# Range checks moved to GpSimd bytes, a searched instruction order, and fewer halved output tiles in a fused attention and mixture kernel

## The chip, the core and the metric

The kernel runs on one core of a Trainium2 chip. The core has TensorE (PE; its weight loads are listed as PEld), VectorE (DVE), ScalarE (ACT), GpSimd (POOL), and SyncE (SP), on whose queue nearly all transfers are issued. The metric is device time of one execution in microseconds (us), lower is better. All arithmetic that matters here is float32, or fp32r on TensorE.

## What is computed

Three layers run one after the other: attention with two kinds of mask, a soft mixture of eight experts, and a layer `g = h - tanh(h)` between two weight matrices.

```python
# attention: 4 batches, 8 heads, 576 tokens, head size 64; x becomes [2304, 512]
scores = where(mask[h], q @ k.T / 8, -1e9);  x = softmax(scores) @ v
# soft mixture: 8 experts, 4 slots each
logits = x @ phi                              # [2304, 32]
slot_input = softmax(logits, axis=0).T @ x    # [32, 512]
slot_out[e] = relu(slot_input[e] @ w1[e]) @ w2[e]
x = softmax(logits, axis=1) @ slot_out        # [2304, 512]
# last layer
h = x @ w_in                                  # 2304 x 2048
out = (h - tanh(h)) @ w_out                   # 2304 x 512
```

All inputs are stored as 64-bit floats, so a piece of 128 by 512 weights is a load of 512 KB and has to be narrowed on the chip.

## The kernel before

The work lies in three stretches. **Attention** runs first (up to about 121 us). While it runs, half of the last layer's weights (eight pieces of `w_in`, called i0 to i7, and eight of `w_out`, o0 to o7) are loaded and narrowed. **Dispatch, experts and combine** follow (to about 181 us); they stream the expert weights through recycled buffers. `dispatch` ends with two PSUM copies into `ct` (L745, L746) on DVE, and behind them on DVE stand the two copies of the slot inputs (L1295) for which the first expert matmul waits.

The **second stage** (`second`, L876) is the last layer. The output of the mixture is a product of a 2304 by 32 matrix `cT` and `soT`, so for each of 16 blocks `f` of the hidden layer it makes a small factor `Gs` (L974 to L992), then `h = Gs * cT` for a group of up to four 128-token tiles (L1106), then on ACT a square `u` (L1110), then the polynomial `r = (h + b) * u`. That is one DVE instruction (L1117), or, for a third of the blocks (`POOLR`), an ACT copy `d` (L1121) and a GpSimd product (L1125). Each tile then adds `r * wh[f]` to its PSUM accumulator (L1079). A further matmul of `cT` with the matrix `Ms` is added once per tile (`affine`). `Ms` needs every piece of `w_out`.

Tiles 0 to 17 are grouped as A (0 to 3), BG (4 to 7), C (8 to 11), DG (12 to 15), EG (16, 17). The list `phases` (L879) says in which order groups are worked, over which blocks, and where their sums go. `"part"` copies the accumulator of the first eight blocks to SBUF (`store`, L1156). `"add"` adds it to the second half on DVE (L1174). `"out"` is a plain copy by ACT or DVE (L1168). Before the change A, BG and EG are worked in halves, which is ten tiles.

The remaining 16 pieces (`loads`) arrive during the second stage. Each is narrowed by `low` (ACT L269 or GpSimd L271), `top` (GpSimd L274) and `merge` (DVE L279). Once the last one is merged, all 32 pieces are loaded **again** (L1259), only to find out whether any exponent was outside the range for which the fast path is right: `check` (L896) is one DVE instruction for each piece, on the top 16 bits of 512 elements, and a last `sift`, a matmul `marks` and some tiny DVE instructions (`judge_*`) make a flag. If the flag is set, a slow general path runs behind the end; with these inputs it doesn't. The buffers of raw pieces are 12 (`RAW`).

The order of instructions on every engine in the second stage is not written by hand. `Plan.run` (L91) is a list scheduler: each task has an engine and an estimated duration, the scheduler takes among the tasks that could start first the one with the longest chain behind it, and the emitted order is the order of estimated start times. Transfers of pieces are a task of an engine "DMA", output writes one of an engine "OUT"; the queue of SP on which both are issued is not a resource of its own. There are 3 PSUM buffers for `h`, 4 accumulators, 3 `u`, 2 `d`, and 5 `r`.

Of the kernel before, what the change touches and what calls it, by code (L numbers as in the profile page):

```python
# [13 lines left out]
I16 = mybir.dt.int16  # L14
BF16 = mybir.dt.bfloat16
# [26 lines left out]
WROUND = 2.0 ** -15 - 0.5  # L42
WHUGE = float(np.uint32(1151 << 20).view(np.float32))
# [33 lines left out]

class Plan:
# [12 lines left out]
    def run(self, free_at):  # L91
        tasks, free_at = self.tasks, dict(free_at)
        users, users_left, left, order, released = [[] for _ in tasks], [0] * len(tasks), {}, {}, {}
# [6 lines left out]
        for tag, keys in self.ordered.items():  # L100
            for k in range(self.bufs[tag], len(keys)):
                t = takes[tag, keys[k]]
                t["deps"] = t["deps"] + [g for g in gives[tag, keys[k - self.bufs[tag]]] if g not in t["deps"]]
        for t in tasks:
            t["dur"] = min(sum(p[1] for p in a) for a in t["alts"])
            for d in t["deps"]:
                users[d["id"]].append(t)
            users_left[t["id"]] = len(t["deps"])
            for x in t["free"]:
                left[x] = left.get(x, 0) + 1  # L110
        sorted_, wait = [t for t in tasks if not t["deps"]], list(users_left)
        for t in sorted_:
            for u in users[t["id"]]:
                wait[u["id"]] -= 1
                if not wait[u["id"]]:
                    sorted_.append(u)
        assert len(sorted_) == len(tasks)
        for t in reversed(sorted_):
            t["rank"] = t["dur"] + max((u["rank"] + 0.2 for u in users[t["id"]]), default=0.0)
        open_, emits, taken = [t for t in tasks if not t["deps"]], [], {}  # L120

        def after(d, t):
            if d["eng"] == t["alts"][0][0][0]:
                return 0.0 if d["eng"] == "PE" else 0.05
            return 0.35 if d["eng"] == "PE" else 0.15

        def earliest(t):
            s = t["ready"]
            for d in t["deps"]:
                s = max(s, d["end"] + after(d, t))  # L130
            for tag, key in t["take"]:
                k = order.get(tag, [])
                if tag in self.ordered and self.ordered[tag][len(k)] != key:
                    return None
                s = max(s, taken.get(tag, -99.0))
                if len(k) >= self.bufs[tag]:
                    old = (tag, k[len(k) - self.bufs[tag]])
                    if old not in released:
                        return None
                    s = max(s, released[old] + 0.2)  # L140
            return s

        while open_:
            found = []
            for t in open_:
                s = earliest(t)
                if s is None:
                    continue
                best = None
                for a in t["alts"]:  # L150
                    x, at = s, []
                    for eng, dur, _ in a:
                        x = max(x, free_at[eng])
                        at.append(x)
                        x += dur + 0.15
                    if best is None or x < best[0]:
                        best = (x, a, at)
                found.append((best[2][0], t, best))
            assert found, "no task can start"
            first = min(f[0] for f in found)  # L160
            s, t, (x, a, at) = max((f for f in found if f[0] <= first + 0.06), key=lambda f: f[1]["rank"] + f[1]["boost"])
            for (eng, dur, emit), b in zip(a, at):
                free_at[eng] = b + dur
                emits.append((b, len(emits), emit))
            t["end"], t["eng"] = at[-1] + a[-1][1], a[-1][0]
            for tag, key in t["take"]:
                order.setdefault(tag, []).append(key)
                taken[tag] = at[0]
            for x in t["free"]:
                left[x] -= 1  # L170
                t.setdefault("frees", []).append(x)
                self.ends = getattr(self, "ends", {})
                self.ends[x] = max(self.ends.get(x, 0.0), t["end"])
                if not left[x]:
                    released[x] = self.ends[x]
            open_.remove(t)
            for u in users[t["id"]]:
                users_left[u["id"]] -= 1
                if not users_left[u["id"]]:
                    open_.append(u)  # L180
        assert all("end" in t for t in tasks)
# [13 lines left out]
def attention_moe_moe(ctx: ExitStack, tc: tile.TileContext, q, k, v, phi, w1, w2, w_in, w_out, cst, out, dbg=None):  # L195
# [489 lines left out]
    def dispatch(pa, ps, ct):  # L685
# [59 lines left out]
        nc.vector.tensor_copy(ct[:, 0:4].rearrange("p c b s -> p c (b s)"), tps[:, 0:4])  # L745
        nc.vector.tensor_copy(ct[0:64, 4].rearrange("p b s -> p (b s)"), tps[0:64, 4])  # L746
# [129 lines left out]
    def second(raw, chk, cT, store, more, wh0):  # L876
# [9 lines left out]
        seen = chk.tile([128, 512], U16, name="seen")  # L886
        counted = []
# [4 lines left out]
        def check(piece):  # L892
            if not counted:
                nc.vector.tensor_scalar(out=seen, in0=quarter(piece, 3, U16), scalar1=0x7800, scalar2=0x3800, op0=ALU.bitwise_and, op1=ALU.bitwise_xor)
            else:
                nc.vector.scalar_tensor_tensor(out=seen, in0=quarter(piece, 3, U16), scalar=0x3800, in1=seen, op0=ALU.bitwise_xor, op1=ALU.bitwise_or)  # L896
            counted.append(piece)
# [23 lines left out]
        plan = Plan(dict(raw=RAW, h=3, p=1, acc=4, u=3, r=5, d=2, g1=2, o=8))  # L921
# [6 lines left out]
        DMA = 1.36  # L928
        for x in PRE:
            P["ld", x] = P["mg", x] = add(one("DMA0", 0.0, lambda: None), ready=-99.0)  # L930
        for k, piece in enumerate(PRE + loads):
# [7 lines left out]
            else:  # L939
                ld = add(one("DMA", DMA, lambda piece=piece: load(piece)), take=[("raw", piece)], ready=at - 1)  # L940
                ld = add(one("DMA0", 0.0, lambda: None), deps=[ld], ready=0)
# [3 lines left out]
            if k >= 0:  # L945
                lo = add(one("ACT", 0.88, lambda piece=piece: low(piece, True)), one("POOL", 1.1, lambda piece=piece: low(piece, False)), deps=[ld] + busy)
            if k >= 0:
                tp = add(one("POOL", 0.87, lambda piece=piece: top(piece)), deps=[ld] + busy)
            if k < 0:
                mg = P["ld", piece]  # L950
            else:
                mg = add(one("DVE", 0.85, lambda piece=piece: merge(piece)), deps=[ld, lo, tp], free=[("raw", piece)])
            P["mg", piece] = mg
            if kind == "o":
# [3 lines left out]
                P["wh", f] = add(one("POOL", 1.1, lambda f=f: nc.gpsimd.tensor_scalar(out=whi(f), in0=place(("o", f)), scalar1=8.0, scalar2=0.0, op0=ALU.mult, op1=ALU.add)),  # L958
# [493 lines left out]
```

## Time and profile before

| | us |
|---|---|
| median of the runs (3 runs) | 306.13 (305.60 to 306.23) |
| the profiled execution, device time | 307.51 |
| its span, first to last instruction | 305.7 |
| around the span | 1.8 |

| engine | busy us | share of the span |
|---|---|---|
| PE | 280.3 | 92% |
| DVE | 223.8 | 73% |
| ACT | 153.3 | 50% |
| POOL | 150.3 | 49% |

Shares are of the whole span, over three stretches with different limits, so they don't say which engine holds a stretch. A matmul's recorded duration is longer than the distance between the starts of two in a row, so PE's busy time overstates its work and hides some of its idle time. In a timeline row, the number in brackets is the idle time of the engine before the row, and behind the arrow is what ended it. A row with a count and one duration is a run of like instructions, first start to last end.

### The profile page before, as it was taken

The numbers are of one execution on the slowest core, as the hardware profiler recorded it, in microseconds if no ns is written. First come the engines' busy times: TensorE is split into PE (matmuls) and PEld (weight loads), VectorE is DVE, ScalarE is ACT, GpSimd is POOL, SyncE is SP. The second block draws the span as 40 slices with busy tenths as digits, with TensorE's granted clock in tenths as the row PEclk, the third lists the DMA queues.
The fourth block names the chain that finished last, engine by engine and source line by source line (L and its number), as shares of the span: only waits on it lengthen the run. The fifth ranks groups of instructions, "written<-read, shape, count | busy, mean of one in ns | idle before, by whom it ended". The sixth has DMA issues, their size and how long they took to land.

```text
span 305.7 us, 7472 instructions
## 1 busy us (share of the span) xinstructions
PE 280.3 (92%) x2684; PEld 193.4 (63%) x2684; DVE 223.8 (73%) x720; ACT 153.3 (50%) x289; POOL 150.3 (49%) x215
## 2 busy tenths in 40 slices
PE   5999999999899999989999876999999999998980
PEld 2688877878578877643333223677746787776750
DVE  5567988775979886526513109999999989999990
ACT  3356646546264455402212038797767348767530
POOL 8627957856789570010634028899370323323310
PEclk9999999999999999999999999999999999999997
DMA  7979899979897989999999999986471399984004
GB/s 206 249 200 347 236 341 307 346 219 300 261 352 207 346 289 399 411 407 373 385 408 409 407 393 397 409 280 207 144 209 61 90 390 396 383 324 139 0 0 147
DMA packets 62698, 86.94 MB, mean 284 GB/s; under 512 B 19008, under 2 KB 48064, under 8 KB 62656
## 3 DMA queue, kind: packets, MB, share of 16 engines
q1 hardware_dynamic: 61568, 86.15, 81.1%
q8 instruction: 23, 0.38, 0.5%
q10 hardware_dynamic: 1088, 0.26, 0.4%
q14 instruction: 19, 0.16, 0.2%
HBM read 81.67 MB, written 4.72 MB: 283 GB/s over the span
## 4 chain that ended last, share of the span: by engine, by line
PE 53%; DVE 15%; DMA 15%; POOL 5%; issue 5%; ACT 4%; SPq 1%; ACTq 0%; POOLq 0%; DVEq 0%
PE acc L1079 17%; PE sc L465 6%; PE pv L495 4%; PE h L1106 4%; PE pp L484 4%; DMA X<-in_moe_w 3%; DMA w<-in_moe_w 3%; DMA raw_o<-in_moe_w_out 3%; DVE seen L896 3%; DVE r L1117 3%; DMA raw_i<-in_moe_w_in 3%; PE xt L410 2%; PE hp L821 2%; PE tr_q L393 2%; PE tr_k L393 2%
## 5 line engine op out<-in xcount | busy, mean ns | idle before, releaser
L1079 PE MATMUL acc<-wh,r 128*128 128x512 f32 x288 | 79.6, 397 | 2.6 <-DVE r L1117 2.1
L1110 ACT ACTIVATE u<-h,co 128x512 f32<-128x512 f32 (+1 forms) x80 | 50.3, 648 | 26.9 <-PE h L1106 23.1
L1079 PEld LDWEIGHTS acc<-wh,r 128*128 128x128 f32 x288 | 52.7, 188 | 15.6 <-POOL X L274 1.9
L1125 POOL TENSOR_TENSOR r<-d,u 128x512 fp32r<-128x512 f32 (+1 forms) x22 | 27.6, 1255 | 49.6 <-PE acc L1079 25.5
L1117 DVE SCALAR_TENSOR_TENSOR r<-h,co,u 128x512 fp32r<-128x512 f32 (+1 forms) x58 | 38.6, 691 | 0.3
L465 PE MATMUL sc<-kT,qT 64*64 64x96 f32 (+1 forms) x608 | 34.2, 252 | 0.7 <-DVE kT L402 0.4
L469 DVE CUSTOM_DVE_ANT_0 sm<-sc,m_sb 128x96 f32<-128x96 f32 x144 | 29.2, 257 | 6.3 <-PE sc L465 6.2
L485 ACT ACTIVATE pT<-pp 96x512 f32<-96x512 f32 x38 | 23.1, 607 | 19.3 <-PE pp L484 19.3
L1106 PE MATMUL h<-cT,Gs 128*128 128x512 f32 (+1 forms) x80 | 29.6, 392 | 3.3 <-DVE r L1117 1.8
L465 PEld LDWEIGHTS sc<-kT,qT 64*64 64x64 f32 x608 | 26.9, 133 | 5.1 <-issue 1.8
L360 POOL TENSOR_SCALAR vw<-vw 32x256 f32<-32x256 f32 (+1 forms) x40 | 27.1, 678 | 4.6 <-DMA vw<-in_v 1.9
L495 PE MATMUL pv<-vw,pT 97*64 97x65 f32 x608 | 26.1, 227 | 0.1
L495 PEld LDWEIGHTS pv<-vw,pT 97*64 97x64 f32 x608 | 20.8, 137 | 7.7 <-issue 6.3
L403 ACT COPY qT<-tr_q 128x512 f32<-128x512 f32 x16 | 13.6, 851 | 23.6 <-PE tr_q L393 23.6
L484 PE MATMUL pp<-c_sb,sm 128*96 128x128 f32 x152 | 23.7, 278 | 1.5 <-DVE sm L473 0.9
L473 DVE TENSOR_TENSOR sm<-sm,mx 128x384 f32<-128x384 f32 (+1 forms) x38 | 22.5, 591 | 1.2
L1106 PEld LDWEIGHTS h<-cT,Gs 128*128 128x128 f32 x80 | 14.8, 188 | 13.5 <-DVE r L1117 6.7
L419 ACT COPY xT<-xt 128x512 f32<-128x512 f32 (+1 forms) x19 | 14.0, 758 | 11.5 <-PE xt L410 10.9
L484 PEld LDWEIGHTS pp<-c_sb,sm 128*96 128x96 f32 x152 | 15.8, 126 | 5.9 <-DVE sm L473 2.1
L274 POOL TENSOR_SCALAR pre<-raw_o 128x512 bf16<-128x512 int16 x16 | 13.7, 859 | 10.2 <-DMA raw_o<-in_moe_w_out 9.9
L279 DVE SCALAR_TENSOR_TENSOR pre<-raw_o,pre 128x512 int32<-128x512 int32 x16 | 13.8, 869 | 5.2 <-POOL pre L271 5.2
L896 DVE SCALAR_TENSOR_TENSOR seen<-raw_o,seen 128x512 uint16<-128x512 uint16 x16 | 17.3, 1080 | 0.3
(214 smaller groups left out, 484.5 us busy)
## 6 DMA issues: line engine op xcount, KB each, us to landing
w<-in_moe_w SPq DMA_DIRECT2D x54, 512.0 KB, 9.6
raw_i<-in_moe_w_in SPq DMA_DIRECT2D x32, 512.0 KB, 7.2
raw_o<-in_moe_w_out SPq DMA_DIRECT2D x32, 512.0 KB, 6.4
q<-in_q SPq DMA_DIRECT2D x16, 256.0 KB, 5.0
k<-in_k SPq DMA_DIRECT2D x16, 256.0 KB, 5.2
X<-in_moe_w SPq DMA_DIRECT2D x8, 512.0 KB, 9.4
out<-X SPq DMA_DIRECT2D x14, 256.0 KB, 4.2
vw<-in_v SPq DMA_DIRECT2D x16, 144.0 KB, 4.9
```

The source lines that it names most:

```text
L360: copy = lambda dst, src: nc.gpsimd.tensor_scalar(out=dst, in0=src, scalar1=1.0, scalar2=0.0, op0=ALU.mult, op1=ALU.add)
L465: nc.tensor.matmul(dst[half, lo:hi], lhsT=qT[u % NQ][half, i:i + QB], rhs=keys[half], start=True, stop=True)
L469: nc.vector.tensor_tensor_reduce(out=sm[:, o:o + n, :].rearrange("p g k -> p (g k)"), in0=sc[:, o:o + n, :].rearrange("p g k -> p (g k)"), ...
L484: nc.tensor.transpose(pp[:, i, :], sm[:, i, :], ident)
L485: nc.scalar.activation(out=pT[0:KB], in_=pp, func=AF.Exp, scale=0.125)
L495: nc.tensor.matmul(pv[64 * ab:64 * ab + 64, i, :], lhsT=pT[:, o + x, 64 * ab:64 * ab + 64], rhs=w[:, ab, u % 2, j + x, :], start=x == 0, s ...
L896: nc.vector.scalar_tensor_tensor(out=seen, in0=quarter(piece, 3, U16), scalar=0x3800, in1=seen, op0=ALU.bitwise_xor, op1=ALU.bitwise_or)
L1079: nc.tensor.matmul(live[key], lhsT=lhsT(), rhs=rhs(), start=new, stop=n == due)
L1106: nc.tensor.matmul(live["h", key], lhsT=Gs[:, 128 * f:128 * (f + 1)], rhs=cT[:, c0:c0 + w], start=True, stop=True)
L1110: nc.scalar.activation(out=live["u", key], in_=live["h", key], func=AF.Square, scale=co[:, SC, f:f + 1])
L1117: nc.vector.scalar_tensor_tensor(out=live["r", key], in0=live["h", key], scalar=co[:, BB, f:f + 1], in1=live["u", key], op0=ALU.add, op1=A ...
L1125: nc.gpsimd.tensor_tensor(out=live["r", key], in0=live["d", key], in1=live["u", key], op=ALU.mult)
```

## The change

- **Checks.** A checked piece is first turned into bytes by GpSimd (`code`): the top 16 bits times 2^-11, rounded, 512 int8 values. Four pieces lie side by side in a 2048-byte half of a room (two halves, planned as resource `code` with two buffers), and DVE compares them with one int32 instruction of 512 elements. So there are 32 GpSimd instructions and 8 DVE ones in place of 32 DVE ones. A raw buffer is free once GpSimd has read it. `sift` gets a second instruction.
- **Halves.** `phases` is reordered: A and EG are halved (six tiles); BG is worked over all 16 blocks in one go, and its four sums leave as plain copies. The room of the bytes is the part of `store` that the four halves left.
- **Order.** `Plan.run` becomes a search: the list scheduler (`order`) runs 500 times with randomly disturbed priorities, each order is timed by a model (`replay`) with two sets of stretched durations, and the best is emitted. Durations are smaller than before, gaps between engines are named per engine, and every transfer takes 0.45 us of the engine SP and then time on "BW".
- **Dispatch.** The two copies into `ct` go from DVE to ACT.

```diff
+WCODE = 2.0 ** -12 - 0.5
-        phases = [(A, lo8, "", "part"), (BG, lo8, "", "part"), (EG, lo8, "", "part"), (A, hi8, "last", "add"), (BG, hi8, "last", "add"), (EG, hi8, "last", "add"), (C, range(NF), "first", "out"), (DG, range(NF), "first", "out")]
+        phases = [(A, lo8, "", "part"), (EG, lo8, "", "part"), (BG, range(NF), "last", "out"), (A, hi8, "last", "add"), (EG, hi8, "last", "add"), (C, range(NF), "first", "out"), (DG, range(NF), "first", "out")]
-        seen = chk.tile([128, 512], U16, name="seen")
+        room = store[:, 3072:].bitcast(I8)
+        seen = room[:, 4096:6144].bitcast(I32)
+        some = room[:, 6144:7168].bitcast(F16)
...
-                nc.vector.scalar_tensor_tensor(out=seen, in0=quarter(piece, 3, U16), scalar=0x3800, in1=seen, op0=ALU.bitwise_xor, op1=ALU.bitwise_or)
+        def code(piece, k):
+            nc.gpsimd.tensor_scalar(out=room[:, 512 * (k % 8):512 * (k % 8 + 1)], in0=quarter(piece, 3, I16), scalar1=2.0 ** -11, scalar2=WCODE, op0=ALU.mult, op1=ALU.add)
+        def check(k):
+            t = room[:, 2048 * (k % 2):2048 * (k % 2 + 1)].bitcast(I32)
...
+                nc.vector.scalar_tensor_tensor(out=seen, in0=t, scalar=0x07070707, in1=seen, op0=ALU.bitwise_xor, op1=ALU.bitwise_or)
...
-            nc.vector.tensor_scalar(out=seen, in0=seen, scalar1=0x7800, scalar2=None, op0=ALU.bitwise_and)
+            nc.vector.tensor_scalar(out=seen, in0=seen, scalar1=0x0F0F0F0F, scalar2=None, op0=ALU.bitwise_and)
+            nc.vector.tensor_scalar(out=some, in0=seen, scalar1=1.0, scalar2=None, op0=ALU.min)
...
-            ld = add(one("DMA", DMA, lambda piece=piece: load(piece)), deps=[P["mg", loads[-1]]], take=[key])
-            ld = add(one("DMA0", 0.0, lambda: None), deps=[ld], ready=0)
-            ck = add(one("DVE", 0.8, lambda piece=piece: check(piece)), deps=[ld, ck], free=[key])
+            ld = add(one("SP", 0.45, lambda piece=piece: load(piece)) + one("BW", 1.3, lambda: None), deps=[P["mg", loads[-1]]], take=[key])
+            cds.append(add(one("POOL", 0.67, lambda piece=piece, k=k: code(piece, k)), deps=[ld] + cds[k - (k % 4 or 4):][:1], take=[("code", k // 4)] if k % 4 == 0 else [], free=[key]))
+            if k % 4 == 3:
+                ck = add(one("DVE", 0.9, lambda k=k: check(k // 4)), deps=cds[-4:] + [ck], free=[("code", k // 4)])
...
-                add(one("OUT", 0.7, lambda t=t: write(t, live["o", t])), deps=[z], free=[("o", t)])
+                add(one("SP", 0.45 * len(token_rows(t)), lambda t=t: write(t, live["o", t])) + one("BW", 0.68, lambda: None), deps=[z], free=[("o", t)])
...
+    def run(self, free_at, rounds=TRIALS):
+        rng = random.Random(2)
+        pri = self.link()
+        likely = [[1.0 + 0.1 * rng.uniform(-0.3, 1.0) for _ in self.tasks] for _ in range(2)]
+        def cost(p):
+            done = self.order(p, free_at)
+            return (1e9 if done is None else sum(self.replay(done, free_at, x) for x in likely)), done
+        best, done = cost(pri)
+        for _ in range(rounds):
+            by, share = rng.choice((1, 3, 8, 20)), rng.choice((0.005, 0.02, 0.1, 0.5))
+            p = [x + rng.gauss(0, by) if rng.random() < share else x for x in pri]
+            c, d = cost(p)
+            if c <= best:
+                best, pri, done = c, p, d
...
-        nc.vector.tensor_copy(ct[:, 0:4].rearrange("p c b s -> p c (b s)"), tps[:, 0:4])
-        nc.vector.tensor_copy(ct[0:64, 4].rearrange("p b s -> p (b s)"), tps[0:64, 4])
+        nc.scalar.copy(ct[:, 0:4].rearrange("p c b s -> p c (b s)"), tps[:, 0:4])
+        nc.scalar.copy(ct[0:64, 4].rearrange("p b s -> p (b s)"), tps[0:64, 4])
```

## Rows read from the trace of the kernel before

**Rows 1.** Busy time of each engine by stretch; PEclk, DMA share, GB/s last.
```profile
core 0: us, PE busy (x) PEld busy (x) DVE busy (x) ACT busy (x) POOL busy (x), PEclk, DMA share, GB/s
170.00:180.00 10.00, 8.08 (x39) 1.60 (x37) 0.85 (x4) 0.06 (x1) 0.00 (x0) 1.00 1.04 401
185.50:224.00 38.50, 36.61 (x184) 25.93 (x185) 37.10 (x76) 31.50 (x63) 29.94 (x42) 1.00 0.80 280
224.00:297.40 73.40, 70.45 (x314) 51.35 (x313) 70.87 (x126) 43.77 (x75) 22.44 (x19) 1.00 0.56 199
297.40:305.70 8.30, 0.05 (x1) 0.00 (x0) 0.93 (x3) 0.97 (x2) 0.00 (x0) 0.77 0.40 135
```

**Rows 2.** Waits, 185 to 306 us: total us, times, longest.
```profile
PE acc L1079 <- DVE r L1117: 2.1, 2, 1.5
...
PE h L1106 <- DVE r L1117: 1.8, 2, 1.2
...
PE h L1106 <- DVE Gs L992: 1.3, 1, 1.3
...
PE acc L1079 <- DVE X L1174: 0.5, 1, 0.5
...
PEld msum L1044 <- POOL r L1125: 0.3, 1, 0.3
```

**Rows 3.** One matmul in the page's groups (mean ns); nine in the timeline.
```profile
L1079 PE MATMUL acc<-wh,r 128*128 128x512 f32 x288 | 79.6, 397 | 2.6 <-DVE r L1117 2.1
...
279.55 2.26 PE L1079 MATMUL acc<-wh,r 128*128 128x512 f32 x9
```

**Rows 4.** Instruction groups, 181 to 306 us: count, busy us, mean ns, idle before.
```profile
L896 DVE SCALAR_TENSOR_TENSOR seen<-raw_o,seen 128x512 uint16<-128x512 uint16 x16 | 17.3, 1080 | 0.3
L896 DVE SCALAR_TENSOR_TENSOR seen<-raw_i,seen 128x512 uint16<-128x512 uint16 x15 | 13.8, 919 | 0.2
...
L1174 DVE TENSOR_TENSOR X<-acc,store 128x512 f32<-128x512 f32 x10 | 6.2, 680 | 0.5 <-PE acc L1079 0.5
```

**Rows 5.** Single lines over the whole span: minimum, median, maximum ns.
```profile
L896 DVE SCALAR_TENSOR_TENSOR seen<-raw_o,seen x16: 674/693/1823, 225.7 to 290.3; 128x512 uint16<-128x512 uint16 x16
L279 DVE SCALAR_TENSOR_TENSOR pre<-raw_o,pre x16: 675/693/1790, 32.6 to 220.8; 128x512 int32<-128x512 int32 x16
L274 POOL TENSOR_SCALAR pre<-raw_o x16: 765/774/1219, 30.8 to 208.6; 128x512 bf16<-128x512 int16 x16
L958 POOL TENSOR_SCALAR wh<-pre x5: 618/619/942, 209.9 to 222.3; 128x512 fp32r<-128x512 f32 x5
```

**Rows 6.** Timeline: a check and a GpSimd product that start together.
```profile
274.33 1.29 POOL L1125 TENSOR_TENSOR r<-d,u 128x512 fp32r<-128x512 f32 x1 [4.60 <-PE acc L1079]
274.34 1.82 DVE L896 SCALAR_TENSOR_TENSOR seen<-raw_o,seen 128x512 uint16<-128x512 uint16 x1
```

**Rows 7.** Groups of GpSimd instructions, 224 to 306 us.
```profile
L1125 POOL TENSOR_TENSOR r<-d,u 128x512 fp32r<-128x512 f32 (+1 forms) x16 | 21.1, 1322 | 44.9 <-PE acc L1079 25.5 <-ACT d L1121 15.3 <-PE h L1106 4.0
```

**Rows 8.** Timeline at the start of the second stage.
```profile
184.21 1.14 DVE L279 SCALAR_TENSOR_TENSOR pre<-raw_o,pre 128x512 int32<-128x512 int32 x1
...
185.39 0.50 DVE L992 TENSOR_TENSOR Gs<-p,Gs 64x128 fp32r<-64x128 f32 x2
...
187.65 1.21 DVE L279 SCALAR_TENSOR_TENSOR X<-raw_i,X 128x512 int32<-128x512 int32 x1
...
189.79 0.94 PE L1079 MATMUL acc<-wh,r 128*128 128x512 f32 x3 [1.55 <-DVE r L1117]
```

**Rows 9.** Timeline of the end.
```profile
297.42 3.53 SPq L1062 DMA_DIRECT2D out<-X  x5
...
297.67 0.69 DVE L1168 COPY X<-acc 128x512 f32<-128x512 f32 x1
```

**Rows 10.** Timeline in dispatch, behind the copies into `ct`.
```profile
135.45 0.32 POOL L1293 MEMSET store<- 128x256 f32 x1 [16.70 <-DVE ct L746]
...
135.80 0.36 DVE L1295 COPY store<-sit 128x64 f32<-128x64 f32 x2 [0.79 <-POOL store L1293]
```

More of the change, by code (lines that the diff above doesn't have):

```diff
@@ L1 @@
+import random
 from contextlib import ExitStack
@@ L109, in run, with gap, order @@
+    def gap(a, b):
+        if a == "BW":
+            return 1.6
+        if a == b:
+            return 0.0 if a == "PE" else 0.08
+        return {"PE": 0.22, "ACT": 0.14, "DVE": 0.12, "POOL": 0.08}.get(a, 0.0) + (0.1 if b == "PE" else 0.0)
+    def order(self, pri, free_at):
+        tasks, bufs, users, free_at = self.tasks, self.bufs, self.users, dict(free_at)
+        left, order, released, taken, ends = {}, {}, {}, {}, {}
+        for t in tasks:
             for x in t["free"]:
                 left[x] = left.get(x, 0) + 1
-        sorted_, wait = [t for t in tasks if not t["deps"]], list(users_left)
@@ L112, in run @@
[L112 to L125, printed above, removed]
@@ L127, in earliest @@
-        def earliest(t):
-            s = t["ready"]
-            for d in t["deps"]:
[L130 to L140, printed above, removed]
-            return s
+        wait = [len(t["deps"]) for t in tasks]
@@ L166, in run @@
+                found.append((i, best))
+                first = best[2][0] if first is None else min(first, best[2][0])
+            if not found:
+                return None
+            i, (_, a, b) = max((f for f in found if f[1][2][0] <= first + 0.06), key=lambda f: pri[f[0]])
+            t = tasks[i]
+            for (e, dur, _), x in zip(a, b):
+                free_at[e] = x + dur
+            done.append((i, a, b))
+            end[i], engine[i] = b[-1] + a[-1][1], a[-1][0]
             for tag, key in t["take"]:
@@ L176, in run @@
[L176 to L179, printed above, removed]
-                    open_.append(u)
-        assert all("end" in t for t in tasks)
+                    released[x] = ends[x]
+            open_.remove(i)
+            for u in users[i]:
+                wait[u] -= 1
+                if not wait[u]:
+                    open_.append(u)
+                    at[u] = base(tasks[u])
+        return done
@@ new lines, in replay @@
+    def replay(self, done, free_at, stretch):
+        tasks, bufs, free_at = self.tasks, self.bufs, dict(free_at)
+        left, order, released, ends = {}, {}, {}, {}
+        for t in tasks:
+            for x in t["free"]:
+                left[x] = left.get(x, 0) + 1
+        end, engine, last = [0.0] * len(tasks), [None] * len(tasks), 0.0
+        for i, a, _ in done:
+            t = tasks[i]
+            s = t["ready"]
+            for d in t["deps"]:
+                s = max(s, end[d["id"]] + self.gap(engine[d["id"]], a[0][0]))
+            for tag, key in t["take"]:
+                k = order.setdefault(tag, [])
+                if len(k) >= bufs[tag]:
+                    s = max(s, released[tag, k[len(k) - bufs[tag]]] + 0.2)
+                k.append(key)
+            for e, dur, _ in a:
+                s = max(s, free_at[e]) + dur * stretch[i]
+                free_at[e] = end[i] = s
+                s += 0.1
+            engine[i] = a[-1][0]
+            last = max(last, end[i])
+            for x in t["free"]:
+                left[x] -= 1
+                ends[x] = max(ends.get(x, 0.0), end[i])
+                if not left[x]:
+                    released[x] = ends[x]
+        return last
@@ L951, in second @@
             else:
[L952 removed]
+                mg = add(one("DVE", 0.82, lambda piece=piece: merge(piece)), deps=[ld, lo, tp], free=[("raw", piece)])
             P["mg", piece] = mg
@@ L1155, in second @@
                 if into == "part":
-                    add(one("ACT", 0.6, lambda t=t, k=k: nc.scalar.copy(part(t), live[k])), one("DVE", 0.69, lambda t=t, k=k: nc.vector.tensor_copy(part(t), live[k])), deps=every[t], free=[fk])
+                    add(one("ACT", 0.49, lambda t=t, k=k: nc.scalar.copy(part(t), live[k])), one("DVE", 0.6, lambda t=t, k=k: nc.vector.tensor_copy(part(t), live[k])), deps=every[t], free=[fk])
                     continue
```

149 lines of the change are left out of this document (85 added, 64 removed).

## Prediction

> **What bounds the kernel now.** I read the stretches first, because shares of the whole span mix three stages. In the second stage, from the first `h` matmul to the last sum (185.5 to 297.4 us), two engines are full at once. Before 224 us DVE is busy for 37.1 of 38.5 us and PE for 36.6; after it DVE for 70.9 of 73.4 and PE for 70.5. GpSimd has much to do before 224 us (29.9 us) and little after (22.4 of 73.4 us) [rows 1]. The cut is at 224 us because the first check follows it [rows 5]: the checks lie wholly in the second part.
>
> Then the waits, to see which of the two engines holds the other. PE's waits in the stage are few: 2.1 us and 1.8 us for DVE's `r`, 1.3 us for DVE's `Gs`, 0.5 us for DVE's addition, 5.7 us in all, and it is DVE that ends every one [rows 2]. So PE is nearly full, and where it isn't, DVE is late. PE's idle time is a little larger than the record says: nine matmuls in a row take 2.26 us while one is recorded with 0.40 us, so one starts every (2.26 - 0.40)/8 = 0.23 us [rows 3], and each stall hides another 0.40 - 0.23, some 0.16 us.
>
> This is the main reading: **DVE's load is going to fall by a third, but PE is the next wall and stands only some 6 us away.** The six stalls come to 5.7 + 6 x 0.16 = 6.7 us.
>
> **The checks.** 31 of the 32 old ones took 17.3 + 13.8 = 31.1 us [rows 4]; with the first at their mean it is 32 us. A check alone takes 0.69 us [rows 5]; the means are 1.08 and 0.92, and the reason is seen where one starts with a GpSimd product: it takes 1.82 us against 1.29 for the product [rows 6].
>
> The new DVE compare reads two int32 operands of 512 elements from SBUF, like `merge`: 0.69 at the median, 1.79 at most [rows 5]. I take 0.9 for it, nearer the median since a byte instruction is shorter than a product. Eight are 7.2 us (5.5 to 14.3). `sift` grows by one instruction, between nothing and the 0.69 of a lone check; I take 0.5. DVE after 224 us is then 70.9 - 32 + 7.2 + 0.5 = 46.6 of 73.4 us, less another 2 or so where additions become copies that ACT may do.
>
> The byte instruction isn't in the trace. Nearest is `top`, one input with the same stride, 0.77 us; an instruction with contiguous input takes 0.62 [rows 5]. I take 0.77, since the stride is the same, with 0.62 to 1.22 (the longest `top`) as bounds: 32 x 0.77 = 24.6 us (20 to 39). GpSimd after 224 us then has 22.4 + 24.6 = 47 of 73.4 us. It is no bound by load. But on its queue stand 16 products of 1.32 us on the mean [rows 7] behind which matmuls stand, and each can now wait behind a byte instruction. Today PE waits 0.3 us for them in all [rows 2], and they themselves wait 25.5 us for PE to free a buffer [rows 7]: they are early.
>
> What speaks against moving work to GpSimd is the Trainium skill, SBUF — State Buffer, Who interferes with whom: a DVE instruction with two SBUF inputs and a GpSimd one that reads SBUF take turns on a shared port pair, whole instruction by whole instruction. The long check beside the product agrees [rows 6]. By the rule each of the 8 compares may wait out one byte instruction, 8 x 0.77 = 6.2 us, which DVE's 27 free us would still cover; and the products gain, since 32 old opponents become 8. So the rule doesn't turn the sum round.
>
> **The halves.** BG in one go removes four copies of partial sums and turns four additions of 0.68 us [rows 4] into copies by either engine. PE does the same 288 + 18 sums. It leaves DVE some 2.7 us or more lighter and lets accumulators go sooner; the 0.5 us wait for an addition [rows 2] is counted below. BG reaches block 8 after the same 80 half-sums as A did, so the pieces i8 to i15 are wanted no sooner. The sums of `Ms` come at the same place.
>
> **The order**, stall by stall:
> - *Middle.* Without the start, PE waits 0.6 + 1.8 + 0.5 = 2.9 us in four stalls (2.1 less the 1.55 of the first sum [rows 8], and the others [rows 2]), with 4 x 0.16 = 3.5 us. All are ended by DVE behind checks or additions. With DVE at 64% they go. A new order makes stalls of its own; the old order's are 3.5 at a full DVE, so 0 to 3.5; I take 1.2. Gain 2.3 us (0 to 3.5).
> - *Start.* PE waits 1.3 us for `Gs` [rows 2] and 1.55 for the first `r` [rows 8]. Before each DVE does a `merge`, of 1.14 and of 1.21 us [rows 8]. No check runs here, so relief doesn't help; only an order that puts these two merges later does. Both gone would be an estimated 1.9 us (0.8 for the first, of which `Gs` waits out only a part, and 1.1 for the second). A list scheduler takes what can start now, and random priorities change that only by luck: gain 0.5 (-0.5 to 1.9).
> - *End.* The last copy ends at 297.67 + 0.69 = 298.36, and the last of five output writes leaves the queue at 297.42 + 3.53 = 300.95 [rows 9], 2.6 us later: the four tiles finish together and queue up on SP. Had the first three been written earlier, one write of about 0.45 us (the new plan's figure; here 3.53/5 = 0.7) would follow the copy, at 298.9: 2 us less. The model now has this queue, and DVE is free to make the last `r` early. But the search sees it only as one of many terms: gain 1.0 (0 to 2).
> - *Dispatch.* The slot inputs' copies start at 135.80, on a GpSimd memset which starts at 135.45 [rows 10], 0.44 us after DVE's second `ct` copy. At most 0.4 us is saved. I take nothing: from 170 to 180 us the transfer engines are full (share 1.04, 401 GB/s) [rows 1], the stretch ends with the last weights' landing and not with the arithmetic. If that cover were gone it would be 0.4.
>
> Sum: 2.3 + 0.5 + 1.0 + 0 = 3.8 us. The profiled execution took 307.51 us, 1.4 above the median of 306.13, with a span of 305.7; the gain is a difference inside the span, so it is taken off both: 303.7 for a profiled execution like that, and **306.1 - 3.8 = 302.3** for the median.
>
> **Rivals.**
> - *PE is the wall and the search gives little.* The new order has as many stalls as the old, other ones. Only the end gains a little: 306.1 - 0.7 = 305.4 (304.6 to 306.4). For it: PE is busy for 107 of 111.9 us [rows 1], and what is idle sits partly at the start, where nothing is relieved. Against: every stall in the middle has DVE at its end [rows 2].
> - *GpSimd's queue holds the products: slower.* Place: the 16 products after 224 us [rows 7]. A block of four sums and an `h` is about 5 x 0.23 = 1.16 us of PE [rows 3], so a product that is held up by longer than that makes PE wait. One byte instruction of 0.77 fits in, two in a row (1.54) don't: 0.38 us and 0.16 for the restart, 0.54 each. From 7 products on (7 x 0.54 = 3.8) the gain is gone; with all 16 it is 302.3 + 8.6 = 310.9. For it: byte instructions come in fours, and pieces land together. Against: `r` has five buffers, and products wait for PE now [rows 7], not PE for them [rows 2].
> - *The search closes nearly all.* Middle 3.5, start 1.9 and end 2 are 7.4 us: 298.7. Against: model and chip differ by the very contention of rows 6, which the plan doesn't have.
>
> **How the numbers follow.** Forecast 302.3 (its own range 300.2 to 304.5): 0.55. Little gain: 0.18. Slower by GpSimd: 0.15. Nearly all: 0.12. The range leaves out half of the last and most of the slower case: 299.0 to 307.0. A measurement of this kernel can tell about 0.2%, 0.6 us, from no change. Faster by more than that: 0.55 + 0.12 + 0.10 of the little gain = 0.77; within it the other 0.08; slower 0.15.
>
> **What would show it.** In the new profile, DVE should be busy for 43 to 50 us of the last 73 of the stage and GpSimd for 42 to 60; the byte instruction should take 0.62 to 0.8 us alone, the compare 0.7 to 1.2; PE's waits for DVE's `r` after the start should be under 1 us and its span from the first `h` to the last sum 108 to 110 us; the last write should leave the queue within 2 us of the last copy. If PE waits for the GpSimd product by more than 2 us, the slower rival has it. If PE's span doesn't shrink while DVE is idle, I was wrong that DVE makes the stalls. If the stage starts (`h` for block 0) more than 0.5 us sooner, dispatch did count.

## The result, and the profile after

The changed kernel takes 302.74 us (median; before 306.13): a ratio of 0.9887 with an interval of 0.9856 to 0.9917. The profiled execution took 302.03 us with a span of 300.2. A second build of it, which differs by an unused constant, gave 0.9888 (0.9833 to 0.9944).

The part ahead of the second stage ends at a different time in every profile, between 178.1 and 183.3 us, also where its instructions are the same. So I set the profiles side by side at a mark that all have, the copy of `phi` that ACT makes at the head of the second stage, and call the time from there to the end of the span the **stage**.

Single lines, the copy of `phi` in before and in the changed kernel (minimum/median/maximum ns, start in us):

```profile
L858 ACT COPY phi_sb<-sot x1: 265/265/265, 181.3 to 181.3; 128x128 f32<-128x128 f32 x1
```
```profile
L934 ACT COPY phi_sb<-sot x1: 266/266/266, 178.2 to 178.2; 128x128 f32<-128x128 f32 x1
```

From 181.3 to the end at 305.7 are 124.4 us before; from 178.2 to 300.2 are 122.0 us after, and 121.9 in the second build. **The stage is 2.4 us shorter**; the medians differ by 3.4 (by 2.7 in the second build). The 1.0 us between the two isn't in a single pair of profiles. A candidate is the clock: over their executions the median of the mean granted clock is 0.989 to 0.991 for the kernel before and 0.994 and 0.992 for the two builds of the changed one, while the two profiles shown have 0.994 each. That is argued, not shown.

Stretches of the changed kernel, cut as in [rows 1] (busy us of each engine; granted clock, DMA share, GB/s last): the first 39.5 us from the first `h`, and from there to the end of the last sum.

```profile
core 0: us, PE busy (x) PEld busy (x) DVE busy (x) ACT busy (x) POOL busy (x), PEclk, DMA share, GB/s
181.52:221.02 39.50, 36.45 (x181) 25.48 (x182) 34.17 (x69) 30.97 (x62) 31.20 (x41) 1.00 0.76 267
221.02:293.42 72.40, 70.73 (x317) 51.81 (x315) 50.87 (x105) 46.54 (x80) 43.17 (x53) 1.00 0.60 219
```

The same cut for the kernel before:

```profile
185.74:225.24 39.50, 37.85 (x189) 26.74 (x190) 38.04 (x77) 32.40 (x64) 30.86 (x44) 1.00 0.80 280
225.24:297.44 72.20, 69.25 (x310) 50.54 (x308) 69.73 (x124) 42.67 (x72) 21.28 (x17) 1.00 0.55 197
```

DVE is relieved as planned: 69.7 of 72.2 us before, 50.9 of 72.4 after. Yet PE needs 111.9 us from the first `h` to the last sum, where it needed 111.7. What it doesn't work has only moved: 39.50 - 37.85 = 1.65 us before in the first part and 72.20 - 69.25 = 2.95 in the second; after, 3.05 and 1.67. The second part gained 1.3 us, the first, in which no check runs, lost 1.4.

Waits of the changed kernel, 170 to 301 us (total us, times, longest):

```profile
DVE r L1196 <- PE acc L1158: 11.2, 8, 2.2
ACT u L1189 <- POOL r L1204: 7.5, 10, 1.3
PE acc L1158 <- DVE r L1196: 2.4, 3, 1.6
PEld acc L1158 <- POOL r L1204: 1.0, 2, 0.7
PE h L1185 <- ACT d L1200: 0.9, 2, 0.6
PE h L1185 <- DVE r L1196: 0.9, 3, 0.4
```

Against [rows 2], DVE now waits for PE. ACT waits 7.5 us, ten times, for GpSimd's products to free `u`; before that was this line:

```profile
ACT u L1110 <- POOL r L1125: 2.3, 3, 1.7
```

Start and end of the changed kernel in the timeline, which answer to [rows 8] and [rows 9]:

```profile
181.52 0.50 PE L1185 MATMUL h<-cT,Gs 128*128 128x512 f32 x1 [0.17 <-DVE Gs L1071]
...
184.00 0.68 DVE L355 SCALAR_TENSOR_TENSOR X<-raw_i,X 128x512 int32<-128x512 int32 x1
...
185.61 0.94 PE L1158 MATMUL acc<-wh,r 128*128 128x512 f32 x3 [1.59 <-DVE r L1196]
...
291.34 3.06 SPq L1141 DMA_DIRECT2D out<-X  x5
...
293.45 0.59 ACT L1247 COPY X<-acc 128x512 f32<-128x512 f32 x1 [0.28 <-PE acc L1158]
```

The wait for `Gs` is 0.17 us instead of 1.3. The wait for the first `r` is still there, 1.59 us, behind a `merge` again. The last write leaves the queue at 291.34 + 3.06 = 294.40, 0.36 us after the last copy (2.6 before).

### The profile page after: what moved, and what is told of

The parts are those of the page before. It is cut to its first block, busy times and chain, and to the rows that moved or that the text cites. A ratio compares the mean times of both kernels' runs of the same rounds, so it can differ in the third digit from the quotient of the medians.

```text
span 300.2 us, 7509 instructions
## 1 busy us (share of the span) xinstructions
PE 279.4 (93%) x2684; PEld 194.5 (65%) x2684; DVE 199.9 (67%) x689; ACT 155.2 (52%) x293; POOL 170.4 (57%) x247
## 5 line engine op out<-in xcount | busy, mean ns | idle before, releaser
L1204 POOL TENSOR_TENSOR r<-d,u 128x512 fp32r<-128x512 f32 (+1 forms) x22 | 26.9, 1223 | 22.4 <-ACT d L1200 7.0
L1185 PE MATMUL h<-cT,Gs 128*128 128x512 f32 (+1 forms) x80 | 28.2, 387 | 2.0 <-ACT d L1200 0.9
L436 POOL TENSOR_SCALAR vw<-vw 32x256 f32<-32x256 f32 (+1 forms) x40 | 25.2, 629 | 4.4 <-DMA vw<-in_v 1.3
L603 DVE TENSOR_TENSOR X<-pv,rd 128x256 f32<-128x256 f32 (+3 forms) x52 | 16.5, 339 | 1.0
L897 PE MATMUL hp<-w,store 128*32 128x512 f32 x120 | 14.9, 596 | 1.2 <-DVE store L1374 1.2
```

Source lines behind the costliest of these rows:

```text
L436: copy = lambda dst, src: nc.gpsimd.tensor_scalar(out=dst, in0=src, scalar1=1.0, scalar2=0.0, op0=ALU.mult, op1=ALU.add)
L1185: nc.tensor.matmul(live["h", key], lhsT=Gs[:, 128 * f:128 * (f + 1)], rhs=cT[:, c0:c0 + w], start=True, stop=True)
L1204: nc.gpsimd.tensor_tensor(out=live["r", key], in0=live["d", key], in1=live["u", key], op=ALU.mult)
```

## The experiments

My theory after this profile, ORDER in the texts below: the checks were not what held PE; the order was, and the checks' new form pays only with an order that knows how long SP's queue takes. Rivals: the search alone made the gain (any order that it draws would); or the relief of DVE made it, and the search nothing (RELIEF); or GpSimd's queue costs as much as DVE's relief brings, so that a version without GpSimd's products would be faster than either kernel.

All runs in one table. "Ratio" is to the kernel before on the same chip, with its interval; "stage" as above; "idle" is PE's idle time in the first 39.5 us from the first `h` and from there to the last sum, worked out as above; "DVE" its busy time in the latter stretch.

| run | median us | ratio | stage us | idle us | DVE us |
|---|---|---|---|---|---|
| before | 306.13 | | 124.4 | 1.65, 2.95 | 69.7 of 72.2 |
| changed | 302.74 | 0.9887 (0.9856-0.9917) | 122.0 | 3.05, 1.67 | 50.9 of 72.4 |
| e5 same again | 303.25 | 0.9888 (0.9833-0.9944) | 121.9 | 3.06, 1.69 | 50.9 of 72.3 |
| e1 order only | 305.26 | 0.9994 (0.9960-1.0029) | 124.5 | 3.52, 2.04 | 67.8 of 73.6 |
| e2 order, halves | 308.38 | 1.0101 (1.0048-1.0153) | 126.7 | clock, 2.46 | 65.7 of 74.1 |
| e3 checks, halves | 311.55 | 1.0188 (1.0129-1.0247) | 129.6 | 1.81, 7.99 | 52.3 of 78.0 |
| e4 halves only | 304.76 | 0.9991 (0.9954-1.0028) | 125.2 | clock, 2.22 | 67.1 of 73.0 |
| e6 no search | 305.96 | 0.9991 (0.9946-1.0036) | 124.7 | clock, 3.05 | 49.6 of 73.7 |
| e7 seed 3 | 305.41 | 0.9971 (0.9921-1.0021) | 122.2 | 3.30, 0.67 | 47.7 of 70.0 |
| e8 no SP in the plan | 315.22 | 1.0301 (1.0253-1.0349) | 132.1 | 3.39, 8.57 | 46.4 of 83.2 |
| e9 no checks | 301.83 | 0.9823 (0.9768-0.9877) | 118.4 | 2.10, 0.07 | 42.6 of 67.9 |
| e10 old order, no product | 306.37 | 0.9999 (0.9962-1.0035) | 125.8 | 1.58, 3.24 | 54.5 of 72.8 |
| e11 no product | **298.27** | 0.9745 (0.9697-0.9792) | 115.8 | 0.85, 0.01 | 51.9 of 64.9 |
| e12 4000 trials | 302.57 | 0.9839 (0.9793-0.9884) | 121.4 | clock, 0.22 | 47.6 of 71.3 |

"clock" stands where TensorE's clock fell in the first part and its busy time can't be compared (last section). In the second part it was 0.98 in e3, e4 and e10 and 0.92 in e8 (1.00 in the others); matmuls at a lower clock take longer there, so PE's idle time in these four looks smaller than it is. Medians are on different chips and are compared through the ratios. Each kernel has one profile, but two of the changed kernel (the second is e5) differ by 0.1 us in the stage.

**One part at a time.** e1: the changed kernel with the old ten tiles and the old checks on DVE, so the new search alone (its `ct` copies stayed on ACT).

```diff
-        phases = [(A, lo8, "", "part"), (EG, lo8, "", "part"), (BG, range(NF), "last", "out"), ...
+        phases = [(A, lo8, "", "part"), (BG, lo8, "", "part"), (EG, lo8, "", "part"), (A, hi8, "last", "add"), ...
-            cds.append(add(one("POOL", 0.67, ... code(piece, k)), ...
+            ck = add(one("DVE", 0.69, lambda piece=piece: check(piece)), deps=[ld, ck], free=[key])
```

> The new searched order with its new durations, on the old checks (32 DVE instructions), the old ten halved tiles and the old copies into ct's place. Theory ORDER (the gain is made by the order, at the start and at the end of the second stage, and not by DVE's relief): ratio to before 0.990 to 0.993, about 303.5 us; from the end of the ACT copy into phi_sb to the first sum 7.4 us (before 8.5), and from the last sum to the end of the span 6.8 us (before 8.3). Theory RELIEF (the gain comes from DVE's lighter load): ratio 0.997 or more, above 305.2 us, and DVE busy for over 65 of the last 73 us of the stage with PE waiting for r.

The order alone brings nothing that can be told (0.9994), where theory ORDER wanted 0.990 to 0.993, though PE's idle time in the second part falls to 2.04 us with DVE still busy for 67.8 of 73.6 us. The first part takes it back (3.52 against 1.65).

e2: the same with the changed kernel's `phases`; e4: the kernel before with only that line.

> The changed kernel with the old checks: 32 DVE instructions of 512 16-bit elements, no byte instruction on GpSimd; order search, halves and copies into ct as changed. Theory ORDER: within 0.5 us of the changed kernel, 302.3 to 303.5 us, ratio 0.988 to 0.991. Theory RELIEF: it loses the relief and with it 2.3 us or more: 305 us, ratio above 0.995.

> The kernel before with nothing but the new phases: six tiles in halves, BG in one go. Both theories: 305.2 to 306.7 us, ratio 0.997 to 1.002, for its relief of DVE is 3 us at most; ORDER says nothing at all, RELIEF up to 0.8 us from the addition that PE waited for.

The halves alone: nothing (0.9991). With the new order and the old checks: 1.0% slower, on the side of RELIEF and against ORDER. e2 differs from the changed kernel by the form of the checks alone, and its stage is 126.7 - 122.0 = 4.7 us longer. How much of that is the relief isn't shown: e2's order is another draw, and its head has a lower clock (PE is busy for 39.20 of the first 39.5 us, for 36.45 in the changed kernel).

e3: the kernel before with bytes and halves, with its own scheduler (loads planned as one "DMA" resource, no search).

```diff
-            ck = add(one("DVE", 0.8, lambda piece=piece: check(piece)), deps=[ld, ck], free=[key])
+            cds.append(add(one("POOL", 0.77, lambda piece=piece, k=k: code(piece, k)), deps=[ld] + ...
+            if k % 4 == 3:
+                ck = add(one("DVE", 0.9, lambda k=k: check(k // 4)), deps=cds[-4:] + [ck], ...
```

> The kernel before with the byte checks and the six halved tiles, but with the old list scheduler, its old durations, and no search. Theory ORDER: 305.5 to 306.7 us, ratio 0.998 to 1.002, although DVE falls to some 47 busy us of the last 73. Theory RELIEF: 303 to 304.3 us, ratio 0.990 to 0.994, with PE's waits for r gone.

1.9% slower, which neither theory had. Its waits, 179 to 306 us:

```profile
PEld acc L1085 <- POOL r L1131: 6.8, 4, 5.1
PE acc L1085 <- POOL r L1131: 5.7, 2, 4.6
POOL store L896 <- DMA raw_i<-in_moe_w_in: 5.5, 4, 3.2
POOL store L896 <- DMA raw_o<-in_moe_w_out: 5.1, 3, 3.3
```

GpSimd's byte instructions wait 10.6 us for their pieces, and PE waits 5.7 us for GpSimd's products. Bytes with the ten old tiles weren't tried: the bytes' room isn't free beside them.

**What the model of SP's queue is worth.** e8: the changed kernel, search and all, but loads and writes are planned without SP's 0.45 us.

```diff
-            ld = add(one("SP", 0.45, lambda piece=piece: load(piece)) + one("BW", 1.3, lambda: None), ...
+            ld = add(one("BW", 1.3, lambda piece=piece: load(piece)), ...
-                add(one("SP", 0.45 * len(token_rows(t)), ...write...) + one("BW", 0.68, lambda: None), ...
+                add(one("OUT", 0.7, ...write...), ...
```

> The changed kernel with the search, but a planner to which SP's queue is no resource: loads go to the transfer engine and writes to one of their own, as in the kernel before. Theory QUEUE (byte instructions on GpSimd stand waiting for pieces whose loads are late in SP's queue, with products behind them): stage 125 us or more, GpSimd's byte instructions waiting for transfers by 5 us or more, PE waiting for GpSimd's product by 2 us or more, 305 us or more. Rival (durations and search matter, the queue doesn't): 302 to 303.5 us, stage 121.5 to 123 us.

3.0% slower, the stage 10 us longer than the changed kernel's, as theory QUEUE has it. Waits of e8, 179 to 314 us, and the longest stall in its timeline:

```profile
POOL store L970 <- DMA raw_o<-in_moe_w_out: 8.0, 6, 2.6
...
PE acc L1158 <- POOL r L1204: 5.6, 2, 4.7
...
POOL store L970 <- DMA raw_i<-in_moe_w_in: 4.6, 5, 2.4
```
```profile
246.67 0.48 ACT L1200 ACTIVATE d<-h,co 128x256 f32<-128x256 f32 x1
...
248.91 0.65 POOL L970 TENSOR_SCALAR store<-raw_o 128x512 int8<-128x512 int16 x1 [2.56 <-DMA raw_o<-in_moe_w_out]
250.15 0.64 POOL L970 TENSOR_SCALAR store<-raw_i 128x512 int8<-128x512 int16 x1 [0.60 <-DMA raw_i<-in_moe_w_in]
251.46 0.63 POOL L970 TENSOR_SCALAR store<-raw_i 128x512 int8<-128x512 int16 x1 [0.67 <-DMA raw_i<-in_moe_w_in]
...
252.88 0.64 POOL L970 TENSOR_SCALAR store<-raw_i 128x512 int8<-128x512 int16 x1 [0.79 <-DVE store L977]
253.60 0.72 POOL L1204 TENSOR_TENSOR r<-d,u 128x256 fp32r<-128x256 f32 x1
254.38 1.22 PE L1158 MATMUL acc<-wh,r 128*128 128x512 f32 x2 [4.73 <-POOL r L1204]
```

The product's `d` is ready at 246.67 + 0.48 = 247.15. Ahead of the product on GpSimd's queue stand four byte instructions. The first three wait for their own pieces, the fourth for a compare on DVE that frees its half of the room. The product starts at 253.60, 6.45 us late, and PE stands for 4.73 us. Of the 6.45 us the bytes' work is 2.6, the waiting for transfers 1.76 + 0.60 + 0.67 = 3.0, and the waiting for the compare 0.8. PE's other long stall, 3.83 us, ends with ACT's `d`; ACT had waited for a product behind two byte instructions that waited 2.42 and 1.31 us for their pieces. The two stalls are all of PE's 8.57 us idle in the second part but 0.01.

With the queue in the plan (the changed kernel, e6, e7 and e12), no byte instruction is listed as waiting for a transfer. e8's plan differs by the queue alone and e6 makes no search, so it is the queue in the plan that takes these waits away.

**What the search is worth.** e6 emits the first list order (`TRIALS = 0`), e7 starts the search from `Random(3)`, e12 makes 4000 trials.

> The changed kernel with TRIALS = 0: its list scheduler with the new durations, gaps and SP queue, but no search. Theory MODEL (knowing the SP queue and true durations is what lets the byte checks pay): 302.5 to 304 us, stage 122 to 123.5 us. Theory SEARCH (the 500 trials make the gain): 305 us or more, stage 124.5 us or more, with single stalls of PE over 1 us in the middle.

> The changed kernel with another random seed (3 for 2), so another order of nearly the same modelled time. If the modelled time is a fair guide: 302 to 303.5 us, stage 121.5 to 123 us. If the result hangs on the draw: more than 1.5 us away, as the searched order with old checks and halves was (stage 126.7 us).

> The changed kernel with 4000 trials in place of 500 (same seed, so its first 500 are the same). If the modelled time is a guide down to a few tenths: stage 121 to 122 us, 301.5 to 303 us. If what is left is not in the model: 122 us or more, no faster than the changed kernel.

Without the search nothing is gained (0.9991), as theory SEARCH has it, although DVE is busy for only 49.6 of 73.7 us: PE's idle time in the second part, at a full clock, is 3.05 us, that of the kernel before. The longest stall of e6 there, in its waits:

```profile
PE acc L1158 <- DVE X L1253: 1.8, 1, 1.8
```

That addition stands on DVE behind a row of small `judge` instructions, at a place that the order gave it. Some of the stage's 124.7 us is the lower clock at its head (PE is busy for 108.7 us up to the last sum, 107.2 in the changed kernel). With 4000 trials PE's idle time there falls to 0.22 us, but the ratio (0.9839) can't be told from that of 500 trials; here too the clock falls at the head. Another seed has a stage as short (122.2) and yet a ratio of 0.9971; its interval just overlaps that of the same chip's e5, and why the ratio and the stage disagree is open. So by the ratios two draws lie 0.8% apart, nearly as much as the whole change, but that the draw makes this difference isn't shown.

**What the checks still cost.** e9 leaves out the loop of checks with its loads.

> The changed kernel without the second loads, the byte instructions and the compares (it leaves out the range check of the weights; the flag is made from the other tests). Its order is drawn anew. Theory WALL (TensorE's own work and the start hold the stage; the checks, once well placed, cost next to nothing): stage 121 to 122.5 us (changed kernel 122.0), from the first sum to the last 106.5 to 107.8 us. Rival (the checks still cost through DVE, GpSimd or the shared order): stage under 120 us, the sums in under 105.5 us.

Theory WALL falls: the stage is 122.0 - 118.4 = 3.6 us shorter, and PE is idle for 0.07 us in the second part. So some 3.6 us of the stage still hang on the checks and on their 32 transfers; the two weren't separated. e9's order is a new draw too, but the three draws of the changed kernel (122.0, 122.2, 121.4 us in changed, e7, e12) lie within 0.8 us of each other.

**What GpSimd's products cost.** e11 is the changed kernel with all products on DVE, so that GpSimd has only its narrowing and the bytes, and ACT makes no `d` copies; e10 is e3 with the same edit.

```diff
-    POOLR = lambda p, f: p >= 1 and f % 3 == 1
+    POOLR = lambda p, f: False
```

> The byte checks and six halves under the old list scheduler, as in the run of that kind (stage 129.6 us, 113.0 us from the first to the last sum), but with every product r on DVE, none on GpSimd, so nothing of the sums' chain stands on GpSimd's queue behind a byte instruction. Theory QUEUE (byte instructions that wait for pieces hold up products): the stalls of PE behind GpSimd (5.7 us) go, 108 us or less between the sums, stage 125 us or less, although DVE has 22 more instructions. Rival (the old order is bad for another reason, or DVE's load matters): 111 us or more between the sums.

> The changed kernel with every product r on DVE and no copy d on ACT: DVE gets 22 instructions of 0.66 us, ACT loses 22 of 0.58, GpSimd has only its narrowing and its bytes. If DVE's load doesn't hold the stage and the chain through ACT and GpSimd costs stalls: stage 120.5 to 122 us, 301 to 303 us. If DVE becomes the wall again (51 + 12 of 72 us plus unevenness): stage 123.5 us or more.

e10 takes e3's 1.9% back, and from the first to the last sum it needs 107.9 us (113.0 in e3), as theory QUEUE has it. Its waits, 179 to 306 us, and its longest stall:

```profile
POOL store L896 <- DMA raw_o<-in_moe_w_out: 18.9, 11, 10.4
...
POOL store L896 <- DMA raw_i<-in_moe_w_in: 9.2, 9, 1.4
...
DVE store L903 <- POOL store L896: 6.9, 3, 3.9
```
```profile
264.54 0.63 POOL L896 TENSOR_SCALAR store<-raw_i 128x512 int8<-128x512 int16 x1 [1.37 <-DMA raw_i<-in_moe_w_in]
265.21 0.69 DVE L903 SCALAR_TENSOR_TENSOR store<-store 128x512 int32<-128x512 int32 x1 [3.95 <-POOL store L896]
265.81 1.40 DVE L1123 SCALAR_TENSOR_TENSOR r<-h,co,u 128x512 fp32r<-128x512 f32 x2
...
266.62 0.50 PE L1112 MATMUL h<-cT,Gs 128*128 128x512 f32 x1 [2.54 <-DVE r L1123]
```

The byte instructions wait for transfers longer than ever, 28.1 us, and no product stands behind them. That shows the mechanism of e3 and e8 from the other side, but the waiting isn't free: it has moved one engine on. The compare on DVE waits for the bytes, `r` stands behind the compare, and PE waits for `r`. This stall of 2.54 us and another of 0.69 (at 243.89, behind the compare before) are all of PE's 3.24 us idle in the second part but 0.01, though DVE is busy for only 54.5 of 72.8 us. The time is that of the kernel before: in e10 the relief of DVE gives nothing while an instruction with an open wait stands ahead of `r`.

**e11 beats both kernels: 298.27 us**, 0.9745 (0.9697 to 0.9792). Stretches of e11:

```profile
184.26:223.76 39.50, 38.65 (x196) 27.23 (x200) 37.69 (x82) 30.96 (x59) 25.94 (x41) 1.00 0.79 275
223.76:288.70 64.94, 64.93 (x297) 49.21 (x289) 51.85 (x112) 34.61 (x58) 18.97 (x28) 1.00 0.62 220
```

In the second part PE is idle for 0.01 of 64.94 us. DVE carries the products that GpSimd had and is still far from full, 51.9 us. ACT has 34.6 us to do instead of 46.5 in a like stretch, since the `d` copies are gone. Whether the products' place or the `d` copies mattered more wasn't separated. The stage is 6.2 us shorter than the changed kernel's and 8.6 shorter than before's; e11 is one draw, but this is well beyond the 0.8 us among the draws of the changed kernel, and neither expectation had a stage so short.

## Why the prediction was right, and where not

The time came out at 302.74 where 302.3 was forecast, 3.4 us of gain for 3.8, but this is in part luck: **the largest term of the sum was wrong, and other gains made up for it**. The middle gave nothing where 2.3 us were forecast; start and end gave 1.1 and 1.5 where 0.5 and 1.0 were forecast, which makes the stage's 2.4; the last 1.0 us of the median stands in no profile. The interval is 0.3% to either side, not the 0.2% that I took for a measurement.

- **Middle, 2.3 forecast: the failed step.** From the first to the last sum it is 107.3 us before and 107.4 after. I read "all are ended by DVE" as "DVE's load is the cause", and let the stalls go "with DVE at 64%". DVE did fall, to 50.9 of 72.4 us, but e6 and e10 have DVE at 49.6 and 54.5 and PE idle for 3.05 and 3.24 us, as before's 2.95; e1 and e2 have DVE nearly full and 2.04 and 2.46. In these runs the relief helps only together with a search: searched orders with it have 1.67, 0.67 and 0.22 us (changed, e7, e12). What a late item stands behind in the order sets PE's idle time, not DVE's load alone. Within the second part the gain is 1.3 us; that it was lost again in the first part, from 1.65 to 3.05 us, I had not priced. The searched orders with checks and with products on GpSimd (changed, e1, e7, e8) have 3.05 to 3.52 there, e9 without checks 2.10, e11 without products 0.85; why the search pays there isn't shown.
- **"If PE's span doesn't shrink while DVE is idle, I was wrong that DVE makes the stalls"**: that is what happened, 111.9 us after 111.7. The 108 to 110 forecast weren't reached; PE's waits for `r` after the start were 2.4 - 1.59 + 0.9 = 1.7 us where I wanted under 1.
- **Start, 0.5 forecast, 1.1 measured.** The first `h` stands 181.52 - 178.2 = 3.3 us behind `phi` (4.4 before), since the `merge` of 1.14 us that stood ahead of `Gs` on DVE [rows 8] now comes later:

```profile
180.39 0.75 DVE L355 SCALAR_TENSOR_TENSOR X<-raw_i,X 128x512 int32<-128x512 int32 x1 [0.37 <-ACT X L345]
...
181.17 0.29 DVE L1071 TENSOR_TENSOR Gs<-p,Gs 64x128 fp32r<-64x128 f32 x1
```

That is the order, as the prediction had it: in e6, without the search, and in e2, another draw, the merge still stands there and the first `h` comes after 4.9 us. The wait for the first `r` stayed. The first sum is 7.4 us behind `phi` (8.5 before), but 10.9, 10.3 and 10.0 in e1, e7 and e11, which do other work first. Start and middle must be read together: 115.8 us before, 114.8 after, 117.2 in e1, 114.3 in e7, 109.4 in e11.
- **End, 1.0 forecast, 1.5 measured** (8.65 to 7.17 us from the start of the last sum). The queue gave 2.2 us, but from the last write to the end of the span it now takes 300.2 - 294.4 = 5.8 us, where it took 305.7 - 300.95 = 4.75: half is given back in the landing, which the sum left out. My reason for the gain, that the plan now knows the queue, isn't shown: e8, without it, ends in 6.5 us, e6, without the search, in 7.1. It hangs on the order drawn.
- **Dispatch, nothing forecast, nothing found.** The slot inputs' copies start 1.87 us after the `sit` matmul before (133.93 to 135.80) and 1.86 after:

```profile
134.17 0.32 POOL L1372 MEMSET store<- 128x256 f32 x1 [16.69 <-PE sit L820]
...
134.51 0.35 DVE L1374 COPY store<-sit 128x64 f32<-128x64 f32 x2 [3.15 <-POOL store L1372]
```

The memset now waits for the `sit` matmul, not for the `ct` copies that [rows 10] names. By the prediction's sign, the first `h` more than 0.5 us sooner, dispatch would have counted, for it comes at 181.52 instead of 185.74; but the part ahead scatters by 5 us, so the sign can't tell. With the `ct` copies on DVE (before, e3, e4, e10) it ends at 178.5 to 181.3 us, with them on ACT at 178.1 to 183.3.

- **Prices.** The groups of the changed kernel, 178 to 301 us:

```profile
L970 POOL TENSOR_SCALAR store<-raw_i 128x512 int8<-128x512 int16 x16 | 12.0, 750 | 1.3
L970 POOL TENSOR_SCALAR store<-raw_o 128x512 int8<-128x512 int16 x16 | 10.8, 675 | 2.5 <-DVE store L977 1.3
...
L977 DVE SCALAR_TENSOR_TENSOR store<-store 128x512 int32<-128x512 int32 x7 | 5.6, 805 | 3.3 <-POOL store L970 3.2
```

The byte instruction takes 0.71 us on the mean ((12.0 + 10.8)/32) where 0.77 was taken, the compare 0.81 where 0.9 was. DVE is busy for 50.9 us where 43 to 50 was the band, GpSimd for 43.2 in a band of 42 to 60.
- **The rule on the shared port.** The Trainium skill, SBUF — State Buffer, Who interferes with whom, has DVE instructions with two SBUF inputs and GpSimd ones that read SBUF take turns. The 7 compares of the row above average 805 ns against 693 for a lone check [rows 5], and only one is long (1.42 us; the median is 0.69); all that they exceed it by is 7 x 0.11 = 0.8 us, where the prediction's worst reading of the rule was 6.2. It was no bound here.
- **The rival of GpSimd's queue** was real: it is what e3 and e8 show, and the plan's model of SP is what held it off in the changed kernel. I put its price at half a microsecond for each held product, by the bytes' own durations. The cost is their waiting more than their work: in the longest stalls of e8 and e3 a ready product stood for 6.45 and 7.2 us, of which 3.0 and 4.4 were waits for transfers and 2.6 and 2.6 work. In the second part PE is idle for 7.99 and 8.57 us in e3 and e8, against 2.95 in before, whose scheduler e3 has, and 1.67 in the changed kernel, whose checks e8 has. I had the 16 products and the byte instructions on one queue, but not that a byte instruction *waits*. My argument against, that products wait for PE today, failed there: such lead is gone once an instruction with an open wait stands ahead.
- **The rival "PE is the wall"** fell with e11: the stage had 8.6 us to give, 6.4 of it before the last sum, near the 6.7 us of stalls that I took for the limit. The wall is where I put it; what stood before it was the products on GpSimd or the `d` copies that come with them, which the prediction never questioned.

## What to carry to other kernels

A releaser that ends every stall is the engine on which the late item stood; it is the cause only if relieving it moves the waiter. Try a relief by itself before pricing it: here it gave nothing in e6 and e10, nor did the search without it in e1, while both together paid in the changed kernel. When work that waits for transfers is moved to an engine, look at what is queued behind it there, and behind whatever waits for it on the next engine: keep nothing urgent in either place, or plan the transfers with the time their issue takes. And where the emitted order is the outcome of a random search, compare several draws: here two seeds gave 0.9888 and 0.9971.

## What the runs showed of the hardware

**TensorE's clock fell at the head of the stage in four orders** (e2, e4, e6 and, with 0.72 from 189 to 195 us, e12), though the same matmuls run there. Stretches of e6:

```profile
180.10:182.10 2.00, 1.14 (x8) 0.70 (x7) 2.00 (x3) 1.27 (x6) 1.92 (x2) 1.00 1.08 408
182.10:184.10 2.00, 1.12 (x5) 0.81 (x6) 1.87 (x8) 1.40 (x2) 1.86 (x4) 1.00 1.07 386
184.10:186.10 2.00, 1.94 (x10) 1.12 (x8) 1.93 (x6) 1.94 (x5) 1.94 (x3) 0.65 1.06 403
186.10:188.10 2.00, 1.07 (x3) 0.83 (x3) 1.87 (x4) 1.46 (x3) 1.86 (x3) 0.50 1.09 396
```

The granted clock goes from 1.00 (2.4 GHz) to 0.50 (1.2 GHz) after two stretches in which PE was busy for 1.14 and 1.12 of 2 us. In the changed kernel the same place has:

```profile
180.20:182.20 2.00, 1.83 (x12) 1.22 (x11) 1.68 (x6) 1.20 (x6) 1.88 (x3) 1.00 1.07 405
182.20:184.20 2.00, 1.82 (x11) 1.22 (x9) 1.87 (x7) 1.95 (x5) 1.87 (x3) 1.00 1.07 388
```

There it stays at 1.00, and also in the next stretch, in which PE is busy for 0.59 of 2 us. No rule follows: the kernel before kept 1.00 with 1.15, 1.56 and 0.94 busy there, and e7 with 1.17, 0.84 and 0.87. But in e2 and e6 it belongs to the order and not to one execution: the mean granted clock is 0.974 to 0.981 in all six executions of e2 and 0.975 to 0.985 in those of e6, against 0.987 to 0.997 in those of the changed kernel. For e4 (0.976 to 0.990) and e12 (0.984 to 0.992) the ranges overlap, so that isn't shown. So the order that a search picks has a price here that its model doesn't know. The clock fell in the second part too: behind PE's stalls of 4.73 and 3.83 us in e8, 4.63 in e3, 2.54 in e10 and 1.96 in e4, 0.50 was granted in a stretch of 2 us or more. In e8, 0.92 was granted on the mean from 224 us to the last sum.
